# Longer unused matmuls, an earlier load of pair 3 and later values of pair 4 in the head of an attention and MLP kernel

## The chip, the core and the metric

The kernel runs on one core of one Trainium2 chip. The metric is the device time of one execution in microseconds (us), as the median of several runs. The core has a matrix engine (TensorE, PE in the profile), a vector engine (VectorE, DVE), an engine for activation functions (ScalarE, ACT), GpSimd (POOL) and SyncE (SP). POOL, SP and ACT can issue DMAs; all of them are served by the same 16 DMA engines of the core.

## The reference

The inputs are q, k and v of shape (8, 8, 576, 64), that is 8 batches, 8 heads, 576 positions and 64 columns, and 16 further keys and values per head (the beacons). All are float32. The result of the attention is laid out as 4608 tokens of 512 columns and goes through two layers of 512 to 2048 to 512 with a leaky ReLU between them.

```python
k_all = np.concatenate([beacon_k, k], axis=2)
v_all = np.concatenate([beacon_v, v], axis=2)
scores = scale * np.matmul(q, k_all.transpose(0, 1, 3, 2))
causal[:, Nb:] = np.triu(np.ones((S, S), dtype=bool), k=1)
scores = np.where(causal, -1000000000.0, scores)
scores = scores - scores.max(-1, keepdims=True)
a = np.exp(scores)
a /= a.sum(-1, keepdims=True) + 1e-09
...
h = x @ w_in
g = np.maximum(0.01 * h, h)
return (g @ w_out).astype(np.float32)
```

## The kernel before

**The units of work.** Attention is done by pairs of heads: 32 pairs, four to a batch, numbered 0 to 31. The keys of a pair, beacons included, are five blocks of up to 128 rows. The scores are computed with the keys on the partitions; ScalarE takes the exponential out of PSUM into a tile `aT`; GpSimd writes zeros over the triangle above the diagonal (`mask`, `triangle`); a further matmul with V, which carries a column of ones, gives the weighted values and their sum at once (`value`, line 342), and VectorE divides. The results are turned into `xT`, which the MLP reads: `moe1` (line 395) is the first layer and `moe2` (line 433) the second. An MLP step is four matmuls of 512 columns.

**An order written by hand.** All five engines run in the order in which the program names the work (`manual_schedule`). The head of the program is a handful of strings of short steps, which `run` reads. The steps that matter here:

- `lG.W` loads queries (W = 0) or keys (W = 1) of pair G into a raw tile (line 145, on POOL's queue). Each descriptor moves 2304 bytes in and 1152 out.
- `VB.C` loads block C of V of batch B (line 200, POOL's queue), `iN` and `oN` half of the weights of the first and the second layer (lines 118 and 124), `NG.W` queries or keys of pair G in natural layout (line 157), all on POOL's queue. V and N move pieces of 128 bytes into SBUF.
- `qG` and `kG` turn the raw tile of pair G on TensorE by 18 small matmuls with the identity (line 229) and copy the result out of PSUM; `TG` turns the natural layout by DMAs that SP issues (line 165).
- `sG.N` is part N of the scores of pair G and its exponential (lines 253 and 262), `mG.N` the masks (line 275), `vG.H` half H of the values, `xG` and `yG` turn the values on TensorE or by SP's DMAs, `u` and `d` are one MLP step of the first or the second layer.
- `wN` is N unused matmuls (line 486), 128 columns each, of a tile `blank` of zeros into a PSUM tile that nobody reads. `WG.H.N` is N unused matmuls of 112 columns (line 492) into spare columns of the tile that `vG.H` will write.

Later scores, from pair 8 on, are packed into full PSUM tiles (`stretch`, line 297), and a loop over timed events interleaves them with the MLP.

**Waits that come from the order.** POOL issues its DMAs in order, and they share eight semaphores in turn, so each DMA on POOL's queue waits until the one eight before it has landed. The issue of the first half of the first layer's weights (`i0`, line 118) is the sixteenth, behind V0.1, the eighth. The masks stand behind `i0` on POOL. The scores use two PSUM tiles, so a score waits for the exponential of the score two before it. TensorE is in order too: in the head, `s2.2` stands behind the turning of pair 3's queries, `q3`, though it does not use them.

Of the kernel before, what the change touches and what calls it, by code (L numbers as in the profile page):

```python
# [15 lines left out]
def kernel(  # L16
# [11 lines left out]
    nc = tc.nc  # L28
# [59 lines left out]
    blank = singles.tile([128, 128], BF16, name="blank")  # L88
# [54 lines left out]
    def load_qk(g, which):  # L143
        b, hp, grp, rows = where(g)
        loaded["qk", g, which] = nc.gpsimd.dma_start(  # L145
            out=raw_of(b, grp)[which][rows],
            in_=(q, k)[which][b, 2 * hp : 2 * hp + 2].rearrange("h (p i) d -> p h i d", i=RI),
        )
# [42 lines left out]
    def load_v_cast(b, c):  # L191
        dst = v_bufs[b % 2]
        lo = 0
        if c == 0:
            nc.gpsimd.dma_start(
                out=dst[0:NB, 0, :, 0:D], in_=beacon_v[b].rearrange("h p d -> p h d")
            )
            lo = NB
        n = ROWS[c] - lo
        nc.gpsimd.dma_start(  # L200
            out=dst[lo : ROWS[c], c, :, 0:D],
            in_=v[b, :, OFF[c] : OFF[c] + n].rearrange("h p d -> p h d"),
        )
# [38 lines left out]
    def score(g, n):  # L242
        qT, kT = qk[g]
        if n == 0:
            probs[g] = a_bufs[g % NA]
        aT = probs[g]
        parts = SCORES[n]
        sc = ps_sc.tile([128, 2, 512], FP32, name="sc", tag="sc")
        c0 = parts[0][3]
        for c, q0, w, col in parts:  # L250
            for par in range(2):
                ps_ = slice(par * 64, par * 64 + 64)
                nc.tensor.matmul(  # L253
                    out=sc[:, par, col - c0 : col - c0 + w],
                    lhsT=kT[ps_, c * 128 : (c + 1) * 128],
                    rhs=qT[ps_, q0 : q0 + w],
                    start=True,
                    stop=True,
                    skip_group_check=True,
                )  # L260
        w = sum(p[2] for p in parts)
        nc.scalar.activation(  # L262
            out=aT[:, :, c0 : c0 + w], in_=sc[:, :, 0:w], func=AF.Exp, scale=0.125
        )
# [3 lines left out]
    def mask(g, part):  # L268
        aT = probs[g]
        for lo, n, rows in MASKS[part]:  # L270
            triangle(aT, lo, n, rows)
# [210 lines left out]

    def unused(n, cols=128):
        ps = ps_one.tile([128, 512], FP32, name="av", tag="one")
        for i in range(n):
            nc.tensor.matmul(out=ps[:, 0:cols], lhsT=blank, rhs=blank[:, 0:cols], start=True, stop=True)  # L486

    def unused_ahead(g, half, n):
        if (g, half) not in avs:
# [17 lines left out]
    def finish(g, eng=0):  # L507
        if eng < 2 and g in xs:
            x_transposes(g, (dve, act)[eng])
        ready[0] = chunks_with(g)  # L510
        if g % NPAIR == NPAIR - 1:
            turn[0] = 1
            held[0] = KEPT

    def run(steps):
        for step in steps.split():
            op, a = step[0], [int(x) for x in step[1:].split(".")] if step[1:] else []
            if op == "s":
                score(*a)
            elif op == "m":  # L520
                mask(*a)
            elif op == "v":
                value(*a)
            elif op == "x":
                finish(*a)
            elif op == "l":
                load_qk(*a)
            elif op == "V":
                load_v_cast(*a)
            elif op == "N":  # L530
                load_natural(*a)
            elif op == "T":
                turn_pair(a[0])
            elif op == "y":
                x_turn(a[0])
            elif op == "q" or op == "k":
                t_q(a[0], 0 if op == "q" else 1, (dve, act)[a[1] if len(a) > 1 else 0])
            elif op == "b":
                beacon_columns(a[0], (dve, act, pool)[a[1]])
            elif op == "u":  # L540
                up()
            elif op == "P":
                moe1_early(*a)
            elif op == "d":
                down()
            elif op == "w":
                unused(*a)
            elif op == "W":
                unused_ahead(*a)
            elif op == "i":  # L550
                load_w_in(a[0])
            elif op == "o":
                load_w_out(a[0])
            else:
                raise ValueError(step)
# [11 lines left out]
    with order:  # L567
        load_first_keys()
        load_beacon_k(0, 2, nc.scalar)
        nc.vector.memset(blank, 0.0)  # L570
        run("l0.0 l1.0")
        make_identity(nc, ident)
        make_ones()
        run("l1.1 l2.0 l2.1 V0.0 V0.1 V0.2 l3.0 l3.1 V0.3 V0.4 l4.0 l4.1 i0")
        make_pads()
        unused(25)
        cast_beacon_k(0, 2, nc.scalar.copy)
        beacon_transposes(0, 2)
        unused(13)
        nc.scalar.copy(out=k_nat0[:, :, 0], in_=first_k[:, 0])  # L580
        nc.vector.tensor_copy(out=k_nat0[:, :, 1], in_=first_k[:, 1])
        run("q0.1 k0 w6 s0.0 m0.0 w5 s0.1 q1 s0.2 m0.1 k1 w4 s0.3 m0.2")
        run("w6 s1.0 m1.0 q2 s1.1 k2 w6 s1.2 m1.1 w6 s1.3 m1.2 W0.0.4 s2.0 m2.0 W0.0.4 s2.1 q3 l5.0 l5.1 W0.0.2 s2.2 k3 v0.0 m2.1 s2.3 i1 m2.2 W0.1.4 s3.0 m3.0 v1.0 s3.1 v0.1 s3.2 v1.1 m3.1 l6.0 l6.1 s3.3 x0.1 m3.2")
        run("v2.0 l7.0 l7.1 q4 v2.1 V1.0 V1.1 x1 k4.1 v3.0 v3.1 x2.1 s4.0 s4.1 x3 m4.0 V1.2 V1.3 V1.4 u s4.2 u q5 s4.3 m4.1 m4.2 k5 u o0 u")
        load_beacon_k(2, B, nc.gpsimd)
        run("s5.0 s5.1 m5.0 u u s5.2 s5.3 m5.1 m5.2 o1 u q6 k6 u v4.0 u v4.1 s6.0 s6.1 m6.0 u y4 N8.0 N8.1 u s6.2 s6.3 m6.1 m6.2 u")
        cast_beacon_k(2, B, nc.gpsimd.tensor_copy)
        run("q7 u k7 u v5.0 u v5.1 y5 N9.0 s7.0 s7.1 m7.0 d v6.0 v6.1 d y6 T8 s7.2 s7.3 m7.1 m7.2 N9.1 T9")
        beacon_transposes(2, B)
        run("b8.2 b9.2 b10.2 b11.2 u v7.0 v7.1 d d d d N10.0 N10.1 V2.0 V2.1 V2.2 V2.3 V2.4 d d N11.0 N11.1 x7")  # L590


        CUTS = [(0, 512, 1024, 1536, 1664), (0, 384, 896, 1376, 1664), (0, 224, 736, 1248, 1664)]
        BLOCKS = [((0, 0),), ((0, 1),)], [((0, 2),), ((0, 3), (1, 0))], [((1, 1),), ((1, 2),)], [((1, 3), (2, 0)), ((2, 1),)], [((2, 2),), ((2, 3),)]
        FIRST = 2 * NPAIR

        def block(g0, i):
            for tile in BLOCKS[i]:
                stretch([(g0 + r, CUTS[r][n], CUTS[r][n + 1]) for r, n in tile])

        events = []
        for g in range(FIRST, NG):
            if g > FIRST + 3:
                events.append((g - 3.6, 0, run, ("N%d.0" % g,)))
                events.append((g - 3.1, 0, run, ("N%d.1" % g,)))
            if g > FIRST + 1:
                events.append((g - 2.0, 0, run, ("T%d" % g,)))
            if g > FIRST + 3:
                events.append((g - 1.9, 0, run, ("b%d.2" % g,)))
            events.append((g + 2.25, 3, value, (g, 0)))  # L610
            events.append((g + 2.62, 4, value, (g, 1)))
            events.append((g + 2.63, 5, x_turn, (g,)))
            if (g - FIRST) % 3 == 0:
                for i in range(5):
                    events.append((g + (0.31 if g == FIRST else 0.01) + 0.6 * i, 2, block, (g, i)))
        ends = [FIRST]
        for g in range(FIRST, NG):
            events.append((g + 3.5, 2, finish, (g, 2)))
            if g % NPAIR == NPAIR - 1:
                ends.append(g + 3.5)  # L620
        for b in range(3, B):
            for n in range(NKB):
                events.append((4 * b - 0.9 + 0.3 * n, 6, load_v_cast, (b, n)))
        events.sort(key=lambda e: e[:2])
        first_down[0] = 4
        w, d0 = 0, done1[0] + done2[0]
        for at, _, what, args in events:
            while w + 2 < len(ends) and at > ends[w + 1]:
                w, d0 = w + 1, done1[0] + done2[0]
            todo = 2 * NF * ready[0] - KEPT - d0  # L630
            aim = d0 + todo * (at - ends[w]) / (ends[w + 1] - ends[w])
            while done1[0] + done2[0] < aim and fill():
                pass
            what(*args)
        while done2[0] < NCH * NF:
            fill()
# [30 lines left out]
```

## Time and profile before

| | |
|---|---|
| median of 8 runs | 343.12 us (341.04 to 346.12) |
| the profiled execution | 343.88 us |
| span of its records | 342.2 us, that is 1.7 us less |
| TensorE busy | 331.3 us (97%) |
| unused matmuls of 128 columns (line 486) | 71 |
| DMA engines | busy in nearly every slice until about 257 us |

The times of instructions are given from the start of the span. A busy TensorE is not TensorE at its peak, since matmuls overlap in the records. The granted clock of TensorE over the span is 0.987 of full speed, and all of the missing share is in a short stretch of the head and at the very end.

### The profile page before, as it was taken

How to read it: one execution, taken by the hardware profiler on the slowest of the kernel's cores; microseconds unless marked ns; L12 is line 12 of the kernel's file. 1: busy time of each engine (PE TensorE's matmuls, PEld its weight loads, DVE VectorE, ACT ScalarE, POOL GpSimd, SP SyncE). 2: the span in 40 equal slices, each digit the busy share in tenths (PEclk: the TensorE clock that was granted, in tenths of full speed). 3: DMA queues.
4: the chain of work that ended last, by engine and by line, in shares of the span. 5: the costliest groups of instructions: out<-in, count | busy, mean ns of one | idle time of the engine just before them, and what ended most of it. 6: DMA issues, size and time to landing. Idle time of an engine off the chain costs nothing.

```text
span 342.2 us, 7376 instructions
## 1 busy us (share of the span) xinstructions
PE 331.3 (97%) x2936; PEld 169.7 (50%) x2981; DVE 81.9 (24%) x199; ACT 186.6 (55%) x280; POOL 181.1 (53%) x355
## 2 busy tenths in 40 slices
PE   8799999989999999999999999999999999999995
PEld 7575555434544545454454454544545544444442
DVE  3355334211233113311232113212321220000111
ACT  4867872469645874288347852775447205633300
POOL 8696877959997685398466955682211000000000
PEclk9969999999999999999999999999999999999998
DMA  8999999999999999999999999999220130000021
GB/s 134 127 193 193 122 192 153 198 153 162 160 157 192 161 136 119 147 127 140 120 151 117 123 143 120 148 134 81 83 81 18 25 103 33 0 31 33 31 92 61
DMA packets 154322, 40.16 MB, mean 117 GB/s; under 512 B 144384, under 2 KB 148608, under 8 KB 154288
## 3 DMA queue, kind: packets, MB, share of 16 engines
q0 software_dynamic: 100848, 18.54, 78.6%
q1 hardware_dynamic: 53024, 20.96, 33.0%
q8 instruction: 23, 0.38, 0.5%
q10 hardware_dynamic: 416, 0.20, 0.2%
q14 instruction: 11, 0.09, 0.1%
HBM read 37.22 MB, written 9.44 MB: 136 GB/s over the span
## 4 chain that ended last, share of the span: by engine, by line
PE 87%; DMA 5%; POOL 5%; issue 1%; DVE 0%; ACT 0%; POOLq 0%
PE acc L395 35%; PE acc L433 33%; PE av L342 9%; PE sc L297 6%; DMA v_aug<-in_v_dram 3%; DMA q_raw<-in_q_dram 2%; PE sc L253 2%; POOL v_aug L200 1%; PE tp L229 1%; POOL k_nat L157 1%; POOL aT L275 1%; POOL q_raw L145 0%; POOL q_nat L157 0%; PE tp L364 0%; POOL k_raw L145 0%
## 5 line engine op out<-in xcount | busy, mean ns | idle before, releaser
L395 PE MATMUL acc<-xT,w_in_sb 128*128 128x512 bf16 x552 | 134.8, 379 | 1.2 <-issue 0.2
L433 PE MATMUL acc<-w_out_sb,gT 128*128 128x512 bf16 x555 | 132.3, 379 | 1.2 <-issue 0.2
L402 ACT ACTIVATE gT<-acc 128x512 bf16<-128x512 f32 x144 | 84.6, 607 | 63.6 <-PE acc L395 61.8
L310 ACT ACTIVATE aT<-sc 128x1024 bf16<-128x1024 f32 (+3 forms) x96 | 76.8, 867 | 62.5 <-PE sc L297 58.9
L275 POOL TENSOR_SCALAR_AFFINE_SELECT aT<-aT 128x256 bf16<-128x256 bf16 (+2 forms) x160 | 57.7, 388 | 64.8 <-ACT aT L310 52.9
L433 PEld LDWEIGHTS <-gT 128*128 128x128 bf16 x576 | 53.4, 98 | 61.2 <-issue 2.5
L395 PEld LDWEIGHTS <-w_in_sb 128*128 128x128 bf16 x576 | 52.6, 98 | 60.0 <-issue 2.7
L351 DVE RECIPROCAL rec<-av 128x6 f32<-128x6 f32 (+1 forms) x64 | 12.1, 188 | 142.5 <-PE av L342 142.5
L445 DVE COPY osb<-acc 128x512 f32<-128x512 f32 x35 | 24.2, 691 | 85.0 <-PE acc L433 78.6
L342 PEld LDWEIGHTS <-aT 128*128 128x128 bf16 (+1 forms) x960 | 37.1, 99 | 13.5 <-issue 3.4
L342 PE MATMUL av<-v_aug,aT 128*128 128x65 bf16 (+1 forms) x960 | 41.1, 196 | 0.1
L157 POOL DMA_DIRECT2D k_nat<-in_k_dram x48 | 34.8, 731 | 3.6 <-DMA v_aug<-in_v_dram 2.6
L157 POOL DMA_DIRECT2D q_nat<-in_q_dram x48 | 34.8, 731 | 2.2 <-DMA v_aug<-in_v_dram 0.9
L200 POOL DMA_DIRECT2D v_aug<-in_v_dram x40 | 34.0, 857 | 3.0 <-DMA w_in_sb<-in_moe_w_in_dram 2.7
L352 DVE TENSOR_TENSOR x_nat<-av,rec 128x384 bf16<-128x384 f32 (+1 forms) x64 | 31.4, 491 | 2.2
L262 ACT ACTIVATE aT<-sc 128x1024 bf16<-128x1024 f32 (+3 forms) x32 | 26.5, 879 | 6.6 <-PE sc L253 6.6
L297 PE MATMUL sc<-qT,kT 64*128 64x208 bf16 (+16 forms) x368 | 24.4, 255 | 1.4 <-POOL aT L275 1.1
L297 PEld LDWEIGHTS <-kT 64*128 64x128 bf16 x368 | 12.3, 94 | 20.2 <-issue 16.7
L253 PE MATMUL sc<-qT,kT 64*128 64x80 bf16 (+4 forms) x96 | 10.8, 302 | 0.0
L235 DVE COPY qT<-tp 128x576 bf16<-128x576 bf16 x7 | 5.3, 756 | 17.2 <-PE tp L229 17.2
L486 PE MATMUL av<-blank 128*128 128x128 bf16 x71 | 7.3, 270 | 1.1 <-DVE blank L570 1.1
L451 ACT COPY osb<-acc 128x256 f32<-128x256 f32 x1 | 0.4, 372 | 13.7 <-DVE osb L449 13.7
(44 smaller groups left out, 69.5 us busy)
## 6 DMA issues: line engine op xcount, KB each, us to landing
out_dram<-osb SPq DMA_DIRECT2D x35, 256.0 KB, 2.4
q_nat<-in_q_dram POOLq DMA_DIRECT2D x48, 72.0 KB, 4.2
k_nat<-in_k_dram POOLq DMA_DIRECT2D x48, 72.0 KB, 4.6
v_aug<-in_v_dram POOLq DMA_DIRECT2D x24, 128.0 KB, 5.8
w_in_sb<-in_moe_w_in_dram POOLq DMA_DIRECT2D x2, 1024.0 KB, 11.3
w_out_sb<-in_moe_w_out_dram POOLq DMA_DIRECT2D x2, 1024.0 KB, 12.4
q_raw<-in_q_dram POOLq DMA_DIRECT2D x8, 144.0 KB, 7.9
k_raw<-in_k_dram POOLq DMA_DIRECT2D x7, 144.0 KB, 8.6
```

Of the source, the lines that this page charges most:

```text
L157: nc.gpsimd.dma_start(out=t[:, :, par], in_=(q, k)[which][b, 2 * hp + par].rearrange("(t p) d -> p t d", p=NR),)
L200: nc.gpsimd.dma_start(out=dst[lo : ROWS[c], c, :, 0:D], in_=v[b, :, OFF[c] : OFF[c] + n].rearrange("h p d -> p h d"),)
L262: nc.scalar.activation(out=aT[:, :, c0 : c0 + w], in_=sc[:, :, 0:w], func=AF.Exp, scale=0.125)
L275: nc.gpsimd.affine_select(out=view, in_=view, compare_op=ALU.is_ge, fill=0.0, base=128 - n if lo == 0 else 0, channel_multiplier=-1, patte ...
L297: nc.tensor.matmul(out=sc[:, par, at : at + b - a], lhsT=kT[ps_, c * 128 : (c + 1) * 128], rhs=qT[ps_, q0 : q0 + b - a], start=True, stop= ...
L310: nc.scalar.activation(out=probs[g][:, :, lo:hi], in_=sc[:, :, at : at + hi - lo], func=AF.Exp, scale=0.125)
L342: nc.tensor.matmul(out=avv[:, n, 0 : D + 1], lhsT=aT[0 : ROWS[c], par, a0 : a0 + 128], rhs=va[0 : ROWS[c], c, 2 * hp + par, :], start=(c = ...
L352: nc.vector.tensor_tensor(out=x_nat[:, t0:t1].rearrange("p t e d -> p (t e) d"), in0=avv[:, :, 0:D], in1=rec[:, n0:n1, None].to_broadcast( ...
L395: nc.tensor.matmul(out=acc, lhsT=w_in_sb[:, j, fc * 128 : (fc + 1) * 128], rhs=xT[:, j, i * 512 : (i + 1) * 512], start=(j == 0), stop=(j ...
L402: nc.scalar.activation(out=gT[i][:, fc, :], in_=acc, func=AF.Prelu, alpha=0.01)
L433: nc.tensor.matmul(out=acc, lhsT=gT[i][:, fc, t * 128 : (t + 1) * 128], rhs=w_out_sb[:, fc, :], start=(fc == 0), stop=(fc == NF - 1),)
L445: nc.vector.tensor_copy(out=osb, in_=acc)
```

## The change

Three things change in the head; nothing after pair 7 is touched.

1. The unused matmuls take more columns each. `unused` repeats the 128 columns of `blank` by a step of zero, so that one matmul streams 256, 384 or 512 columns. In place of 71 matmuls with 128 columns there are 23, with their 23 weight loads: 25 x 128 becomes 6 x 512, 13 x 128 becomes 6 x 256, `w6` and `w5` become 2 x 384, and `w4` becomes 1 x 512.
2. The loads of pair 3's queries and keys (`l3.0 l3.1`) stand on POOL's queue ahead of the third block of V (`V0.2`), not behind it. With it, two unused matmuls `W0.0.2` stand ahead of `q3`, not between the keys' load of pair 5 and `s2.2`.
3. The values of pair 4 (`v4.0 u v4.1`) stand behind the first scores of pair 6 (`s6.0 s6.1 m6.0`), not ahead of them.

```diff
     def unused(n, cols=128):
         ps = ps_one.tile([128, 512], FP32, name="av", tag="one")
+        r, w = max(1, cols // 128), min(cols, 128)
         for i in range(n):
-            nc.tensor.matmul(out=ps[:, 0:cols], lhsT=blank, rhs=blank[:, 0:cols], start=True, stop=True)
+            nc.tensor.matmul(
+                out=ps[:, 0 : r * w].rearrange("p (r w) -> p r w", w=w),
+                lhsT=blank,
+                rhs=blank[:, None, 0:w].to_broadcast([128, r, w]),
+                start=True,
+                stop=True,
+            )
...
-        run("l1.1 l2.0 l2.1 V0.0 V0.1 V0.2 l3.0 l3.1 V0.3 V0.4 l4.0 l4.1 i0")
+        run("l1.1 l2.0 l2.1 V0.0 V0.1 l3.0 l3.1 V0.2 V0.3 V0.4 l4.0 l4.1 i0")
         make_pads()
-        unused(25)
+        unused(6, 512)
         cast_beacon_k(0, 2, nc.scalar.copy)
         beacon_transposes(0, 2)
-        unused(13)
+        unused(6, 256)
...
-        run("q0.1 k0 w6 s0.0 m0.0 w5 s0.1 q1 s0.2 m0.1 k1 w4 s0.3 m0.2")
-        run("w6 s1.0 m1.0 q2 s1.1 k2 w6 s1.2 m1.1 w6 s1.3 m1.2 W0.0.4 s2.0 m2.0 W0.0.4 s2.1 q3 l5.0 l5.1 W0.0.2 s2.2 k3 v0.0 m2.1 s2.3 i1 m2.2 W0.1.4 s3.0 m3.0 v1.0 s3.1 v0.1 s3.2 v1.1 m3.1 l6.0 l6.1 s3.3 x0.1 m3.2")
+        run("q0.1 k0 w2.384 s0.0 m0.0 w2.384 s0.1 q1 s0.2 m0.1 k1 w1.512 s0.3 m0.2")
+        run("w2.384 s1.0 m1.0 q2 s1.1 k2 w2.384 s1.2 m1.1 w2.384 s1.3 m1.2 W0.0.4 s2.0 m2.0 W0.0.4 s2.1 W0.0.2 q3 l5.0 l5.1 s2.2 k3 v0.0 m2.1 s2.3 i1 m2.2 W0.1.4 s3.0 m3.0 v1.0 s3.1 v0.1 s3.2 v1.1 m3.1 l6.0 l6.1 s3.3 x0.1 m3.2")
...
-        run("s5.0 s5.1 m5.0 u u s5.2 s5.3 m5.1 m5.2 o1 u q6 k6 u v4.0 u v4.1 s6.0 s6.1 m6.0 u y4 N8.0 N8.1 u s6.2 s6.3 m6.1 m6.2 u")
+        run("s5.0 s5.1 m5.0 u u s5.2 s5.3 m5.1 m5.2 o1 u q6 k6 u u s6.0 s6.1 m6.0 v4.0 u v4.1 y4 N8.0 N8.1 u s6.2 s6.3 m6.1 m6.2 u")
```

## The prediction

> **What bounds the kernel now.** I read the page first: TensorE is busy 97% of the span, so anything that shortens TensorE's work or its idle time counts, and little else does. But the share is a mean. The row of the granted clock has one bad place:
>
> ```profile
> PE 331.3 (97%) x2936; PEld 169.7 (50%) x2981; DVE 81.9 (24%) x199; ACT 186.6 (55%) x280; POOL 181.1 (53%) x355
> ...
> PEclk9969999999999999999999999999999999999998
> ```
>
> The third slice (17.1 to 25.7 us) has 6 tenths. Cut into pieces, the columns being busy time of each engine, then the clock:
>
> ```profile
> 5.70:9.10 3.40, 3.37 (x83) 2.40 (x82) 1.49 (x3) 2.39 (x4) 3.40 (x5) 1.00 1.33 146
> 9.10:12.50 3.40, 3.40 (x75) 2.28 (x70) 2.31 (x4) 3.36 (x6) 3.01 (x5) 1.00 2.01 137
> 12.50:15.95 3.45, 1.78 (x21) 0.88 (x18) 0.00 (x0) 3.07 (x4) 1.23 (x3) 1.00 2.91 125
> 15.95:19.40 3.45, 3.32 (x61) 2.37 (x62) 1.92 (x4) 0.94 (x2) 3.45 (x11) 0.50 1.48 148
> 19.40:22.80 3.40, 3.40 (x40) 2.17 (x40) 1.18 (x4) 2.54 (x3) 3.39 (x8) 0.50 1.11 202
> ```
>
> The third piece is where TensorE is busy only 1.78 of 3.45 us, and just after it the clock is half for 6.8 us. The chain of waits over the first 30 us names what it waits for:
>
> ```profile
> 5.51 2.54 POOL v_aug L200 x3
> 8.05 7.99 DMA q_raw<-in_q_dram
> 16.04 0.04 issue
> 16.08 0.69 PE tp L229 x18
> ```
>
> Pair 3's queries are issued at 8.05 us, behind three blocks of V, and land at 16.04. TensorE idles from 14.28 (end of `s2.1`) to 16.08, 1.8 us. ScalarE runs out at the same time: its ten exponentials end at 15.58 and the next starts at 17.58.
>
> The second thing to see is far behind the change. From 7 us on, the DMA engines always have packets, and TensorE meets them again at the first scores of pair 8 and at 75 us (timeline: start, duration, what, and in brackets the idle time before it; the line with 4.7 is an answer on DMAs, time to landing last):
>
> ```profile
> 57.86 1.20 SPq L165 DMA_TRANSPOSE kT<-k_nat  x1
> ...
> kT<-k_nat SPq DMA_TRANSPOSE x1, 4.7
> ...
> 62.62 0.36 PEld L297 LDWEIGHTS <-kT 64*128 64x128 bf16 x6 [0.59 <-issue]
> ...
> 72.98 1.44 POOL L157 DMA_DIRECT2D k_nat<-in_k_dram  x2 [2.57 <-DMA v_aug<-in_v_dram]
> ...
> 75.50 0.49 PE L297 MATMUL sc<-qT,kT 64*128 64x224 bf16 x6 [1.09 <-POOL aT L275]
> ```
>
> 57.86 + 4.7 = 62.56: pair 8's turned keys land just as TensorE loads them, after 0.59 us of waiting. So at 62.6 us TensorE has no slack towards the DMAs, and at 75.5 it waits 1.09 us more.
>
> **Part 1, longer unused matmuls.** 71 matmuls of 128 columns become 23; 48 matmuls and 48 weight loads go. That is no time by itself: the columns are what costs. The timeline has 25 weight loads of `blank` in 2.59 us at the start, 104 ns each, and at 6.47 us six in 0.34 us, 57 ns each. So a 128-column step takes the time of its columns, first at a slow clock and then at a full one; the weight loads lie beside the matmuls. A matmul of 512 columns with a step of zero is not in the trace; the nearest row is first-layer MLP work, twelve matmuls of 512 columns in 2.59 us, 216 ns each at the full clock, which is four times 54. I take the same price per column; the ends are 6 x 216 = 1.3 us (were the clock full) and 6 x 456 = 2.7 us (the 2.85 us of the matmul row / 25 x 4) against my 6 x 416 = 2.5. Columns: the first two fills go from 38 x 128 = 4864 to 4608, so 256 fewer, 2 x 104 = 0.2 us earlier; the queries of pair 0 landed at 5.34 and are turned at 5.70, so these 0.2 us can be had. `w5` gains 128 columns, +0.05 us, beside the exponentials, which take 8.23 us without a gap from 7.35 and pace everything to 15.58. Sum: **0.15 us** earlier.
>
> **Part 2, pair 3 ahead of V0.2.** Landing times from the answers on DMAs (issue plus time to landing): V0.1 about 14.4, V0.2 15.5, queries 16.04, keys 8.64 + 8.6 = 17.24, V0.3 19.0, V0.4 19.9. They land in the order of issue although issued 0.6 to 0.9 us apart with 8 us of latency, so they stand in one line[...]. Without V0.2 in front, pair 3 saves V0.2's step, 15.5 − 14.4 = 1.1 us: queries at about 15.0, keys at 16.2. V0.2 then lands when all three had landed, 17.24. The ends: 16.04 still (if what holds the line is V0.1's slow engine and the others' traffic), and 0.87 us earlier issue plus the 4.9 us that pair 1 needed in a short line, 12.1. I take 15.0.
>
> TensorE then has `W0.0.2` (0.1 us) and idles about 0.6 us, not 1.8. `s2.2` follows at 15.4, its exponential at 15.8, not 17.58. `k3` ends near 16.7. **The new wait:** `v0.0` needs V0.2 (17.24) and holds the in-order TensorE for 0.5 us, with `s2.3` behind it; before, it started at 18.08, so this is still earlier. V0.3 and V0.4 keep their places: `v0.1` (21.51 before) cannot start its last part before 19.9, and at most 1.6 us are to be had there. On POOL, `i0` waits for V0.1 as before (14.72), so the masks behind it start at 15.50 as before; `v0.0` needs three of them, 16.7. `l5.0` waits on the semaphore of pair 3's queries instead of V0.2's, both long landed by 19.2.
>
> **The clock.** From 16.08 to 22.69 the chain's pieces sum to 6.6 us. The same kinds of pieces after 23 us take: 18 turnings 0.40 (against 0.69), 12 values 0.37 (0.78), 18 values 0.66 (1.10), unused 0.2 (0.49). At a full clock the sum would be 4.0 us, up to 2.6 less, of which V0.4 lets about 1.6 to 2.0 through. Would the clock stay? Here the Trainium skill ("TensorE: Matmul & The Clock Gate", "Why this matters for your kernels") says to avoid idle gaps over about 3 us. By that rule a gap of 1.8 us is harmless, the change touches no cause, and this part is worth the 0.8 us below. The row differs: after 1.78 busy of 3.45 us the clock was 0.50, so the measurement decides that a shorter gap can matter. Against the change speaks Part 4 of the same page, that turning on TensorE does not count as busy: 36 of the small matmuls now in 15 to 17 us are turnings, and the piece 15.95 to 19.40, full by the row (3.32 of 3.45) and rich in them, did not raise the clock. With the clock kept the head gains about 2.0 us, with it lost 0.8 (1.0 earlier, less a wait on V0.2). I take it as even, 1.4 us, plus 0.15.
>
> **Part 3, values of pair 4.** V1.4 is issued at 34.6, lands at 40.3, and `v4.1` starts at 40.12, its last block used near 40.5: slack 0.2. With a head 1.5 us earlier it would wait 1.3 us. The move puts `s6.0 s6.1` (0.58 us) and one MLP step (0.86) ahead, 1.44 us, so the wait goes. POOL's order is the same: `N8` stays behind `m6.0`, whose exponentials come a little sooner. SP's three turnings by DMA (`y4` to `T8`) keep their order. Cost nothing; without it, up to 1.3 us.
>
> **The sum.** TensorE reaches MLP work 1.5 us earlier (28.42 to 26.9; the weights land at 14.72 + 11.3 = 26.0, not late). It keeps that until 62.6 us. There pair 8's keys come from the natural loads issued at 44.5 and landed at 56.9 and 57.3, in line behind the two weight loads, on DMA engines that never ran dry; these do not come sooner, so **TensorE waits away the 1.5 us at 62.6**. What survives is on POOL: its loads from 54.9 on (pairs 9 to 11, V of batch 2) follow masks, so they move ahead with TensorE, and DMA time of a load is only 4 to 5 us there, so the line is short. The 1.09 us of waiting at 75.5, behind V2's landing, can shrink. I take half, 0.6 us. The profiled execution took 343.88; 343.3 after. It stands 0.8 above the median 343.12, so on the median: **342.5 us**.
>
> **Rivals.**
> - *The whole gain is carried* (0.25): the line of DMAs moves up as TensorE does, since POOL's issues after 21 us are tied to masks. For it: latencies fall to 4 us at 57. Against it: packets in every slice. Gain 2.2 us (2.0 + 0.15): 340.9, and 339.4 if other runs are hit harder than the profiled one.
> - *Nothing is gained* (0.16): the clock falls all the same and 62.6 and 75.5 are set by DMA: 343.1.
> - *Slower, V0.2 takes pair 3's place* (0.12): if V0.2 falls back to V0.4's landing, 19.9, `v0.0` starts 1.8 us later than 18.08, TensorE idles 3 us, and one more piece of 3.4 us runs at half clock, 1.7 us. It decides from a landing of V0.2 later than 18.1. 343.1 + 3.5 = 346.6.
> - *The longer fills do not hold the clock*: since columns are equal, I give it no chance of its own; it would show as the second rival.
>
> **How the numbers follow.** The likeliest case (0.47) is the partial gain, 342.5. The range goes from the far end of the first rival, with some room, 339.6, to 345.6, short of the slower one. About 1% is what a measurement of this kernel can tell from no change: under 339.7, over 346.5. Faster by over 1% is only the end of the first rival (0.12); slower most of the last (0.10); within, 0.78.
>
> **What would show it.** Right: queries of pair 3 turned at about 15 us; an idle gap under 1 us ahead of them; `v0.0` waiting on V0.2 near 17.2; first MLP step near 27; idle time before the weight load of pair 8's keys near 2 us instead of 0.59, and less than 1.09 at 75. Wrong: turning still at 16, or keys of pair 8 landing well before 62, which would mean that the DMAs do follow and the gain is whole.

## The result and the profile after

The changed kernel takes **346.47 us** (median of 20 executions, 342.87 to 347.92, one at 560.54 aside) against 343.2 us of 55 executions of the kernel before on the same chip: a ratio of **1.0091**, 95% interval 1.0069 to 1.0114. It is slower by almost 1%, where the forecast was 342.5 us. Ratios here and below rest on undisturbed executions only, so they can differ from the quotient of the two medians shown. The profiled execution took 347.37 us with a span of 345.6 us, 3.4 us more than the span before.

The page of the changed kernel, the rows of busy time and of the granted clock:

```profile
PE 331.9 (96%) x2888; PEld 165.4 (48%) x2933; DVE 81.8 (24%) x199; ACT 186.2 (54%) x280; POOL 181.4 (52%) x355
...
PEclk9999999699999999999999999999999999999999
```

The 48 matmuls are gone and TensorE's busy time is the same. The place with 6 tenths has moved from the third slice to the eighth. The pieces of the head (start and end, length, busy time of PE, PEld, DVE, ACT and POOL, then clock, DMA share, GB/s) have no hole any more where it was:

```profile
12.50:15.95 3.45, 3.45 (x75) 2.21 (x74) 1.27 (x2) 3.45 (x5) 3.45 (x10) 1.00 2.31 135
15.95:19.40 3.45, 3.45 (x72) 2.46 (x69) 2.48 (x9) 3.45 (x6) 3.45 (x8) 1.00 1.28 180
19.40:22.80 3.40, 2.96 (x91) 2.62 (x88) 2.98 (x9) 1.73 (x3) 3.39 (x10) 1.00 1.12 206
```

So the head did what the change says. The timeline of TensorE (start, duration, what) has pair 3's queries turned at 14.17 us with no wait in front, and V0.2 was there for `v0.0` at 15.26:

```profile
14.17 0.47 PE L229 MATMUL tp<-ident,q_raw 64*64 64x64 bf16 x18
14.57 0.35 PE L253 MATMUL sc<-qT,kT 64*128 64x336 bf16 x4
14.86 0.47 PE L229 MATMUL tp<-ident,k_raw 64*64 64x64 bf16 x18
15.26 0.54 PE L342 MATMUL av<-v_aug,aT 128*128 128x65 bf16 x12
```

The first MLP step starts at 24.56 us, 3.9 earlier than in the profile before. This row of the changed kernel, then that of the kernel before:

```profile
24.56 1.08 PE L395 MATMUL acc<-xT,w_in_sb 128*128 128x512 bf16 x3
```

```profile
28.46 1.08 PE L395 MATMUL acc<-xT,w_in_sb 128*128 128x512 bf16 x3
```

All of it is gone by pair 8, and more. A first part goes at 52 us, in a wait for the second half of `w_out`; when TensorE is done with the work ahead of pair 8, at 60.77 us where the kernel before was at 62.53, 1.76 us of the lead are left. The same timeline there and at the first scores of pair 8 (line 297); in brackets the idle time before a row and what ended it:

```profile
53.44 5.34 PE L433 MATMUL acc<-w_out_sb,gT 128*128 128x512 bf16 x23 [1.34 <-DMA w_out_sb<-in_moe_w_out_dram]
...
58.88 1.89 PE L433 MATMUL acc<-w_out_sb,gT 128*128 128x512 bf16 x8
64.59 1.03 PE L297 MATMUL sc<-qT,kT 64*128 64x512 bf16 x6 [3.82 <-DMA kT<-k_nat]
65.56 1.89 PE L433 MATMUL acc<-w_out_sb,gT 128*128 128x512 bf16 x4
67.24 1.91 PE L395 MATMUL acc<-xT,w_in_sb 128*128 128x512 bf16 x4
69.37 1.26 PE L433 MATMUL acc<-w_out_sb,gT 128*128 128x512 bf16 x3 [0.22 <-issue]
70.47 1.03 PE L395 MATMUL acc<-xT,w_in_sb 128*128 128x512 bf16 x4
71.43 0.63 PE L297 MATMUL sc<-qT,kT 64*128 64x16 bf16 x12
```

The first and the second scores of pair 8 in the kernel before:

```profile
62.65 0.61 PE L297 MATMUL sc<-qT,kT 64*128 64x512 bf16 x6
...
66.75 0.64 PE L297 MATMUL sc<-qT,kT 64*128 64x16 bf16 x12
```

In the changed kernel TensorE stands still for 3.82 us in one piece, and an MLP step that takes 1.03 us at 70.47 takes 1.9 us from 65.56 to 69. The pieces show the clock:

```profile
60.00:63.40 3.40, 0.77 (x4) 0.15 (x2) 0.00 (x0) 0.00 (x0) 3.29 (x6) 1.00 1.84 156
63.40:70.30 6.90, 5.49 (x17) 2.05 (x19) 0.00 (x0) 2.54 (x3) 6.24 (x11) 0.51 1.84 193
```

TensorE is busy for 0.77 us of 3.40, and the clock is half for the next 6.8 us, two pieces of 3.4. The sum of the profiled execution: the first scores of pair 8 come 64.59 − 62.65 = 1.94 us later than before; the second ones come 71.43 − 66.75 = 4.68 later, so the stretch at half clock costs 2.74 more; behind them 1.3 us come back, since the wait of 1.09 us at 75.5 is gone. 1.94 + 2.74 − 1.3 = 3.4 us, the difference of the spans.

Why pair 8's turned keys were late is in the chain of waits (start, duration, what):

```profile
40.97 18.18 DMA k_nat<-in_k_dram
59.16 0.00 issue
59.16 0.03 SPq L165
59.19 0.04 issue
59.22 5.23 DMA kT<-k_nat
```

The natural loads were issued 3.9 to 4.2 us earlier than before and were in the line for 18.2 us, not 12.1, so they landed 1.8 us later. The answers on DMAs, first of the kernel before, then of the changed one (last number: us from issue to landing):

```profile
q_nat<-in_q_dram POOLq DMA_DIRECT2D x2, 72.0 KB, 12.5
k_nat<-in_k_dram POOLq DMA_DIRECT2D x2, 72.0 KB, 12.1
```

```profile
q_nat<-in_q_dram POOLq DMA_DIRECT2D x2, 72.0 KB, 18.1
k_nat<-in_k_dram POOLq DMA_DIRECT2D x2, 72.0 KB, 18.2
```

Counted over the packets of the trace, the DMA engines had moved 7.51 MB by 45 us, 0.5 MB more than before; by 60 us they had moved 9.52 MB, a little less than the 9.60 MB of before. In two stretches they moved little:

```profile
40.00:45.00 5.00, 4.89 (x70) 2.63 (x69) 2.03 (x4) 3.54 (x6) 3.09 (x7) 1.00 1.14 192
45.00:48.00 3.00, 3.00 (x56) 1.95 (x54) 1.09 (x5) 2.34 (x3) 2.27 (x4) 1.00 1.68 63
48.00:50.00 2.00, 1.94 (x32) 1.08 (x30) 1.02 (x3) 0.62 (x2) 0.41 (x1) 1.00 1.19 193
...
55.00:57.00 2.00, 2.00 (x11) 0.92 (x10) 0.69 (x1) 0.00 (x0) 0.00 (x0) 1.00 1.77 69
57.00:60.00 3.00, 3.00 (x20) 1.47 (x18) 1.05 (x2) 0.00 (x0) 2.70 (x4) 1.00 2.34 151
```

63 and 69 GB/s, where the pieces beside them have 150 to 195. That was not for want of work: the column ahead of the rate, packets under way per engine, says 1.68 and 1.77 there.

### The profile page after: what moved, and what is told of

Same layout as the page of the kernel before. It is cut to its first block, busy times and chain, and to the rows that moved or that the text cites. A ratio compares the mean times of both kernels' runs of the same rounds, so it can differ in the third digit from the quotient of the medians.

```text
span 345.6 us, 7280 instructions
## 1 busy us (share of the span) xinstructions
PE 331.9 (96%) x2888; PEld 165.4 (48%) x2933; DVE 81.8 (24%) x199; ACT 186.2 (54%) x280; POOL 181.4 (52%) x355
## 4 chain that ended last, share of the span: by engine, by line
PE 82%; DMA 10%; POOL 5%; issue 1%; DVE 0%; ACT 0%; SPq 0%
PE acc L433 34%; PE acc L395 32%; PE av L342 7%; PE sc L297 6%; DMA k_nat<-in_k_dram 5%; DMA w_in_sb<-in_moe_w_in_dram 3%; POOL aT L275 2%; PE av L487 2%; DMA kT<-k_nat 2%; POOL v_aug L200 1%; PE tp L229 1%; PE sc L253 1%; POOL q_nat L157 0%; POOL k_raw L145 0%; POOL w_out_sb L124 0%
## 5 line engine op out<-in xcount | busy, mean ns | idle before, releaser
L402 ACT ACTIVATE gT<-acc 128x512 bf16<-128x512 f32 x144 | 84.7, 607 | 67.2 <-PE acc L395 65.5
L433 PEld LDWEIGHTS <-gT 128*128 128x128 bf16 x576 | 53.7, 98 | 63.8 <-issue 5.8
L395 PEld LDWEIGHTS <-w_in_sb 128*128 128x128 bf16 x576 | 52.9, 98 | 60.4 <-issue 3.6
L351 DVE RECIPROCAL rec<-av 128x6 f32<-128x6 f32 (+1 forms) x64 | 12.1, 188 | 142.2 <-PE av L342 142.2
L342 PEld LDWEIGHTS <-aT 128*128 128x128 bf16 (+1 forms) x960 | 36.3, 98 | 14.3 <-issue 3.0
L253 PE MATMUL sc<-qT,kT 64*128 64x80 bf16 (+4 forms) x96 | 10.1, 284 | 0.0
L487 PE MATMUL av<-blank 128*128 128x384 bf16 (+2 forms) x23 | 7.1, 434 | 1.1 <-DVE blank L577 1.1
```

What stands on the lines that cost most here:

```text
L342: nc.tensor.matmul(out=avv[:, n, 0 : D + 1], lhsT=aT[0 : ROWS[c], par, a0 : a0 + 128], rhs=va[0 : ROWS[c], c, 2 * hp + par, :], start=(c = ...
L395: nc.tensor.matmul(out=acc, lhsT=w_in_sb[:, j, fc * 128 : (fc + 1) * 128], rhs=xT[:, j, i * 512 : (i + 1) * 512], start=(j == 0), stop=(j ...
L402: nc.scalar.activation(out=gT[i][:, fc, :], in_=acc, func=AF.Prelu, alpha=0.01)
L433: nc.tensor.matmul(out=acc, lhsT=gT[i][:, fc, t * 128 : (t + 1) * 128], rhs=w_out_sb[:, fc, :], start=(fc == 0), stop=(fc == NF - 1),)
```

## The experiments

**The theory.** The head gains time, but pair 8's keys come when the DMA line gives them, not sooner. The lead collects there as one wait, and the clock halves behind it, which costs more than the lead is worth. **The rivals:** one of the three parts is slow by itself; part 3 does harm by sending pair 8's loads and the turnings of pairs 5 and 6 into the line earlier; the one profiled execution was unlucky. The last runs add two: the place of TensorE's code loads, and a clock that rises late.

| run | what differs from the kernel before | median us | ratio to before, 95% interval |
|---|---|---|---|
| changed kernel | parts 1, 2, 3 | 346.47 | 1.0091, 1.0069 to 1.0114 |
| e1 | part 1 | 343.82 | 0.9993, 0.9965 to 1.0020 |
| e2 | part 2 | 343.12 | 0.9986, 0.9955 to 1.0018 |
| e6 | part 3 | 343.63 | 0.9978, 0.9951 to 1.0005 |
| e5 | parts 1, 2 | 344.38 | 1.0030, 1.0002 to 1.0059 |
| e15 | parts 2, 3 | 344.08 | 1.0008, 0.9980 to 1.0036 |
| e3 | all, wait at pair 8 filled with unused matmuls | 344.63 | 1.0043, 1.0020 to 1.0066 |
| e4 | all, pairs 5 and 6 turned on TensorE | 341.78 | 0.9959, 0.9936 to 0.9982 |
| e8 | only pairs 5 and 6 turned on TensorE | 342.78 | 0.9985, 0.9960 to 1.0011 |
| e16 | parts 2, 3, pairs 5 and 6 on TensorE | 341.32 | 0.9964, 0.9946 to 0.9982 |
| e11 | all, pairs 4, 5, 6 turned on TensorE | 341.84 | 0.9948, 0.9925 to 0.9971 |
| e7 | all, turnings of pairs 5 and 6 behind pair 8's | 349.10 | 1.0126, 1.0074 to 1.0179 |
| e12 | all, pair 8's loads ahead of half of `w_out` | 348.33 | 1.0161, 1.0113 to 1.0210 |
| e17 | all, opening's unused matmuls as before | 345.25 | 1.0075, 1.0046 to 1.0104 |
| e18 | all, other unused matmuls as before | 346.22 | 1.0035, 0.9998 to 1.0072 |

e9, e10, e13 and e14 are one profiled execution each, told below.

### One part at a time

Part 1 alone, e1 (`unused` as changed):

```diff
-        unused(25)
+        unused(6, 512)
...
-        run("q0.1 k0 w6 s0.0 m0.0 w5 s0.1 q1 s0.2 m0.1 k1 w4 s0.3 m0.2")
+        run("q0.1 k0 w2.384 s0.0 m0.0 w2.384 s0.1 q1 s0.2 m0.1 k1 w1.512 s0.3 m0.2")
...
```

> Part 1 alone (fewer and longer unused matmuls), all else as before. Theory A (the head becomes shorter, TensorE then starves at the first scores of pair 8, which wait for keys that come through the DMA engines at a time of their own, and the long idle time halves the clock for 6.8 us): part 1 moves the head by only 0.2 us, so the time is that of before, 343.2 within 1 us, and the half-clock stretch stays in the head at 16 us. Theory B (the three parts do no harm by themselves; the profiled run met an accidental standstill of the DMA engines of about 3 us at 45 us, and that is what is measured): the same. Theory C (matmuls with a step of zero are themselves the cost): slower, 345 or more.

Part 2 alone, e2:

```diff
-        run("l1.1 l2.0 l2.1 V0.0 V0.1 V0.2 l3.0 l3.1 V0.3 V0.4 l4.0 l4.1 i0")
+        run("l1.1 l2.0 l2.1 V0.0 V0.1 l3.0 l3.1 V0.2 V0.3 V0.4 l4.0 l4.1 i0")
...
```

> Part 2 alone (pair 3's queries and keys ahead of the third block of V, and two unused matmuls ahead of their turning). Theory A: this part alone makes the head 3 to 4 us shorter and so carries the loss: 345.5 to 347, idle time of 3 us or more in front of pair 8's scores at about 64 us and half clock behind it. Theory B: the head is shorter too, and without a standstill the time is at or under that of before, 340 to 343. Theory C: as before, 343.

Part 3 alone, e6, and parts 1 and 2 without it, e5:

```diff
-... o1 u q6 k6 u v4.0 u v4.1 s6.0 s6.1 m6.0 u y4 N8.0 ...
+... o1 u q6 k6 u u s6.0 s6.1 m6.0 v4.0 u v4.1 y4 N8.0 ...
```

> Part 3 alone, the head as before. Theory A2: without the shorter head nothing waits for V at the values of pair 4 (0.2 us of slack in the profile of before), so the move changes little: 342.5 to 344. Theory D (the order of the values of pair 4 is bad by itself, whatever the head): 345 to 347.

> Parts 1 and 2 together, values of pair 4 where they stood before. Theory A2 (part 3 is what turns the shorter head into a loss: without it TensorE waits for the last blocks of V of batch 1 in front of the values of pair 4, some 2 us in small pieces near 38 us, as in the run with part 2 alone, so the turnings by DMA of pairs 5 and 6 are issued later and pair 8's natural loads land sooner): 342.5 to 344, pair 8's keys turned from 55 to 57 us, no wait over 1.5 us there. Theory A (the shorter head alone makes the loss, and the run with part 2 alone was spared by chance): 345.5 to 347.

Each part alone is within the uncertainty of no change. Together they are slower, so the loss is an interaction: no part is slow by itself. Parts 1 and 2 carry about a third of it, and part 3 on top of them the rest (1.0030 to 1.0091). The median of e5, 344.38 us, falls between the two ranges expected for it. Parts 1 and 3 together were not run.

The single profiles do not support the theory as it was put for e1 and e2. In e2 the first MLP step starts at 25.08 us, 3.4 earlier than in the profile before, and 345.5 us or more were expected for that. But 2.0 us go in waits for V at 36 to 38 us, the waits that part 3 was to take away, and the scores of pair 8 follow without any:

```profile
61.82 0.61 PE L297 MATMUL sc<-qT,kT 64*128 64x512 bf16 x6
```

The profile of e1 is that of its slowest execution, 349.04 us, one that its ratio leaves out. Pair 8's natural loads were issued there at 42.7 us as in the kernel before, so they had no lead, and TensorE came to pair 8 later than before, at 63.51. Yet the keys came so late that the same wait stands there, with half clock for one piece behind it:

```profile
67.33 0.61 PE L297 MATMUL sc<-qT,kT 64*128 64x512 bf16 x6 [3.82 <-DMA kT<-k_nat]
```

So in these profiles a lead of the head is neither enough for this wait nor needed for it.

### The wait, and what it does to the clock

e3 keeps the whole change and puts unused work where TensorE would stand still, just ahead of pair 8's first scores:

```diff
+        events.append((FIRST + 0.305, 1, unused, (16, 512)))
```

> The changed kernel with 16 more unused matmuls of 512 columns (16 x 0.216 = 3.5 us at the full clock) right before the first scores of pair 8, that is, inside the wait of 3.8 us. Theory A: the wait for the keys stays, but the clock stays up behind it; the 6.8 us at half clock go, worth about 2.7 us: 343.5 to 344.5 instead of 346.5. Theory B: nothing gained, 346.5, or slower by what the fill overruns. Theory C: 16 more such matmuls make it slower.

The median falls from 346.47 to 344.63 us, just above the 343.5 to 344.5 expected, and the ratio from 1.0091 to 1.0043. In its profile the clock stays full from 5.9 us to the end, and the timeline has a short wait left:

```profile
65.30 0.61 PE L297 MATMUL sc<-qT,kT 64*128 64x512 bf16 x6 [0.72 <-DMA kT<-k_nat]
```

So about half of the loss was the half clock, got back by work that nobody needs. The rest is not told apart: the row of the 16 matmuls has 3.62 us in the profile, so where the keys are not that late, the filling itself costs.

The mean clocks of the single executions agree, though a mean does not tell where the half clock stood. Of 19 executions of the changed kernel 11 have a mean clock of 0.9925 or less (two pieces of 3.4 us at half clock) with a median of 347.25 us, five about 0.995 (one piece) with 345.91, and three 0.998 or more with 343.65. Of 55 of the kernel before in the first set of experiments, 16% are in the first class and 35% in the second; of all 22 of e3 none is under 0.994. Half a clock for 6.8 us is 3.4 us of lost work; 347.25 − 343.65 is 3.6.

### Sparing the DMA engines

e4 turns the values of pairs 5 and 6 on TensorE (`x`), where SP's DMAs did it (`y`); e8 does this alone in the kernel before.

```diff
-... v5.1 y5 N9.0 s7.0 s7.1 m7.0 d v6.0 v6.1 d y6 T8 ...
+... v5.1 N9.0 s7.0 s7.1 m7.0 x5 d v6.0 v6.1 d x6 T8 ...
```

> The changed kernel with the values of pairs 5 and 6 turned by TensorE (0.4 us each on an engine that idles later anyway) instead of by four DMAs of SP, which are in flight between 46 and 60 us together with the natural loads of pair 8. Theory A: less stands in front of pair 8's loads, its keys land 1 to 2.5 us sooner, TensorE waits 1.5 to 3 us instead of 3.8, and where the clock holds the time is 342 to 344. Theory B: the standstill comes or does not come as in the changed kernel, so 346.5 within 1 us.

> The kernel before (none of the three parts) with the values of pairs 5 and 6 turned by TensorE instead of by SP's DMAs. The changed kernel with the same edit took 341.78. If the change has a gain of its own once pair 8's loads are freed, this one lies above it: 342.5 to 343.5, since its head is 3 us longer and TensorE reaches pair 8 at 62 us anyway. If the gain was that of the turning alone: 341.8 within 0.7.

With it the loss is gone: 0.9959 in place of 1.0091, and 341.78 us, under the 342 to 344 expected. Without any of the three parts it is 0.9985; since the two intervals overlap, whether the three parts add to the gain is not shown. In e4's timeline pair 8's transposes leave SP at 52.89, not 57.88, and the scores follow without a wait:

```profile
60.74 0.61 PE L297 MATMUL sc<-qT,kT 64*128 64x512 bf16 x6
```

The clock was full there (0.998 over the span). In all four profiles with these turnings on TensorE (e4, e8, e11, e16) the transposes leave SP between 52.1 and 52.9 us. In the others, but for the three in which the clock rose late (below), they leave between 53.5 and 60.5. e16 is e4 without part 1, e11 turns pair 4 on TensorE as well (`x4`, one MLP step behind the place of `y4`):

> Parts 2 and 3 with pairs 5 and 6 turned by TensorE, the unused matmuls of the head as before. With part 1 the same kernel had a ratio of 0.9959 to before. Theory (part 1 gives a lead that is kept once pair 8's keys are early): 0.9965 to 0.999. Rival (part 1 costs by late lifts of the clock): 0.992 to 0.9955.

> The changed kernel with the outputs of pairs 4, 5 and 6 turned by TensorE (with a vector copy) and not by the DMA engines. Theory (the DMA engines are the bound up to pair 8's keys, and every turning that they are spared brings the keys sooner, at 0.5 to 0.7 us of TensorE for each pair): with pairs 5 and 6 on TensorE the median was 341.8, so a third pair saves little more, since no wait on the keys over 0.7 us is left: 341.2 to 342.3. Rival (TensorE's cost of a turning decides): 342.4 to 343.2.

e16 falls between the two ranges expected: 0.9964 beside 0.9959, so where the keys are early, part 1 is worth nothing that can be seen, neither a gain nor a cost. e11 is where the theory put it, with the lowest ratio of all, 0.9948, though its interval overlaps e4's.

### Moving pair 8 in the line

e7 leaves the turnings to the DMAs but puts those of pairs 5 and 6 behind pair 8's on SP:

```diff
-... v5.1 y5 N9.0 s7.0 s7.1 m7.0 d v6.0 v6.1 d y6 T8 ...
+... v5.1 N9.0 s7.0 s7.1 m7.0 d v6.0 v6.1 d T8 y5 y6 ...
```

> The changed kernel with the turnings by DMA of the values of pairs 5 and 6 behind those of pair 8's queries and keys on SP's queue; same instructions, and TensorE's order is untouched. Theory A2 (it is the early turnings of pairs 5 and 6 that stand between pair 8's loads and their landing): pair 8 is turned from 53 to 55 us instead of 57.9, TensorE's wait falls from 3.8 to under 1.5 us, 341.5 to 343.5. Theory B (a standstill of the DMA engines made the loads late): as the changed kernel, 346.5 within 1 us.

The time missed. The timeline shows that the part on the keys held and that the wait went elsewhere:

```profile
61.09 0.61 PE L297 MATMUL sc<-qT,kT 64*128 64x512 bf16 x6 [0.22 <-DMA kT<-k_nat]
...
65.42 0.55 PE L395 MATMUL acc<-xT,w_in_sb 128*128 128x512 bf16 x1 [2.53 <-DMA xT<-x_nat]
69.31 1.03 PE L395 MATMUL acc<-xT,w_in_sb 128*128 128x512 bf16 x2 [3.35 <-DMA xT<-x_nat]
```

The scores of pair 8 come 3.5 us sooner than in the changed kernel. But the MLP needs what was pushed back, waits 5.9 us for it in two pieces, and the clock is half from 65.5 to 72.3 us. e12 moves the loads themselves:

```diff
-... m5.1 m5.2 o1 u q6 k6 u u s6.0 s6.1 m6.0 v4.0 u v4.1 y4 N8.0 N8.1 u ...
+... m5.1 m5.2 N8.0 N8.1 o1 u q6 k6 u u s6.0 s6.1 m6.0 v4.0 u v4.1 y4 u ...
```

> The changed kernel with the two loads of pair 8's queries and keys issued ahead of the second half of w_out and not five steps behind it. Theory A (the loads land late because everything issued ahead of them has to land first, 18 us in the line): pair 8's turned keys come 3 us or more sooner, first scores of pair 8 without a wait on DMA, and the second half of w_out lands 2 to 4 us later, so that the first down steps wait for it instead: 344 to 348. Theory B (the turnings of pairs 5 and 6 that share the engines set the landing, not the place in the line): the transposes of pair 8 are issued at 56 to 58 as in the changed kernel, 346 to 348 and a wait on kT<-k_nat over 2.5 us.

Theory A is right on the loads, which land in 7.7 and 9.7 us in place of 18, and on the second half of `w_out`, which is late instead:

```profile
59.32 3.15 PE L433 MATMUL acc<-w_out_sb,gT 128*128 128x512 bf16 x7 [4.76 <-DMA w_out_sb<-in_moe_w_out_dram]
```

It is wrong on the keys: their transpose leaves SP 3.5 us sooner than in the changed kernel but is under way for 9.2 us and lands at 64.88, no sooner than there (64.45).

```profile
55.68 2.90 SPq L165 DMA_TRANSPOSE kT<-k_nat  x1
```

No wait is left at pair 8 only because TensorE comes there later, after the wait on `w_out`. The time is just over the 344 to 348 expected.

In both moves another thing became late. Only kernels with transfers taken out of the line (e4, e11, e16) gained anything clear of their intervals. That fits a DMA line that sets the pace up to about 60 us.

### More profiles of both kernels

> The kernel before as it is, for a second profiled execution. Theory: the clock falls to half either in the head (wait for pair 3's queries, 1.8 us in the first profile) or at the scores of pair 8, but not for 6.8 us at the latter; the first scores of pair 8 at 61.5 to 63.5 with a wait under 2 us; 341.5 to 344. Rival (pair 8's keys come as late here as in the changed kernel): first scores of pair 8 at 64 or later.

The kernel before again, 344.33 us: pair 8 at 63.85 us after 1.17 us of waiting, and no half clock before the end, though one was expected in the head or at pair 8.

```profile
63.85 0.61 PE L297 MATMUL sc<-qT,kT 64*128 64x512 bf16 x6 [1.17 <-DMA kT<-k_nat]
```

Its first MLP step stood at 26.87, not 28.46: the half clock in the head of the first profile belongs to that execution.

> The changed kernel as it is, for a second profiled execution. Theory (the head is some 3 us sooner, pair 8's turned keys are not, and the difference stands in one piece ahead of the scores of pair 8): the first MLP step again at 24.5 to 26, the first scores of pair 8 at 63.5 or later after a wait of over 2.5 us on DMA kT<-k_nat, the clock half for 3.4 or 6.8 us behind it, 345 to 348 us. Rival (the one profiled execution was unlucky: the standstill of the DMA engines from 45 to 48 us made pair 8's keys late): without a standstill between 40 and 58 us the keys are there by 62, the wait is under 1.5 us and the time 343 to 344.

> The changed kernel as it is, for one more profiled execution; the second one had TensorE at its lower clock up to 26.9 us and told nothing of pair 8. Theory (the lead of the head stands as one piece of idle time ahead of pair 8): first MLP step at 24.5 to 26, a wait of over 2.5 us on DMA kT<-k_nat, the clock half for 3.4 or 6.8 us behind it, 345 to 348 us. Rival (that wait was the luck of one execution): a wait under 1.5 us, no half clock near 60 to 70, 342.5 to 344.5. Second rival (long unused matmuls leave the clock low for long in the head): full clock first at 10 us or later, first MLP step at 28 or later.

> As the third profile, once more: the first theory holds if at least two of the four profiles of the changed kernel show the wait of over 2.5 us with half clock behind it; the second rival if full clock comes first at 10 us or later in two of them.

Two of the four profiles of the changed kernel, the first and e14, show the wait of over 3 us with half clock behind it. In e14 it was half for one piece, and the time, 344.28 us, was under the 345 to 348 expected:

```profile
63.03 1.04 PE L297 MATMUL sc<-qT,kT 64*128 64x512 bf16 x6 [3.63 <-DMA kT<-k_nat]
```

```profile
62.40:65.80 3.40, 2.77 (x11) 1.04 (x12) 0.00 (x0) 1.94 (x2) 3.20 (x5) 0.50 1.94 166
```

The other two, e9 (346.85) and e13 (346.35), have a quite different trouble: full clock only from 27 us on. The first scores of 512 columns of the changed kernel, then of e9:

```profile
6.69 0.39 PE L253 MATMUL sc<-qT,kT 64*128 64x512 bf16 x2
```

```profile
7.52 0.61 PE L253 MATMUL sc<-qT,kT 64*128 64x512 bf16 x2
```

Their first MLP step comes at 32 us and pair 8's keys are then in time. So both conditions set ahead of e14 are met. The lists of clocks tell that this second trouble is not what the measured 346.47 rests on: no execution there is over 344.9 us at a clock of 0.998 or more, as e9 and e13 are.

### Which part carries it

> Parts 2 and 3 without part 1: the unused matmuls of the head have 128 columns as before. Theory (the head's lead makes the loss, and the lead came of parts 1 and 2 together with the clock kept up): lead about 2 us smaller than in the changed kernel, wait on pair 8's keys 1.5 to 2.5 us, ratio 0.998 to 1.004. Rival (part 3's order of v4 makes the loss, by issuing pair 8's loads and the turnings of pairs 4 and 5 into the line earlier): the changed kernel's loss without part 1, ratio 1.006 to 1.011. Second rival (part 1 alone makes it, by its late lifts of the clock): ratio 0.996 to 0.999.

Parts 2 and 3 alone give 1.0008: **without part 1 there is no loss to be seen**, and part 3's order is not enough for it. Its profile has no wait to speak of at pair 8, where 1.5 to 2.5 us were expected. e17 and e18 take part 1 back by halves:

```diff
-        unused(6, 512)
+        unused(25)
...
-        unused(6, 256)
+        unused(13)
```

> The changed kernel, with only the opening's unused matmuls (before the first queries are turned) back at 25 and 13 of 128 columns: 26 matmuls and 26 weight loads more, no unused work more between scores. Theory A (the lead that the long unused matmuls between the scores give is what stands at pair 8): lead and wait as in the changed kernel, ratio 1.006 to 1.011. Theory B (the place of TensorE's code loads: one of 16 KB for about each 256 instructions of TensorE; with part 1 they fall at 54 to 56 us, where pair 8's loads land and are turned, without it at 51 to 53): 52 instructions more move the loads some 1.6 us ahead, to 44 to 45 and 52.5 to 53, standstills of the DMA engines between 53 and 58 us get rarer, ratio 1.000 to 1.005. Theory C (the long opening leaves the clock low up to 27 us in some executions): no late rise here, ratio 1.000 to 1.005 as with B, but with the code loads' place making no difference in e18.

```diff
-        run("q0.1 k0 w2.384 s0.0 m0.0 w2.384 s0.1 q1 s0.2 m0.1 k1 w1.512 s0.3 m0.2")
+        run("q0.1 k0 w6 s0.0 m0.0 w5 s0.1 q1 s0.2 m0.1 k1 w4 s0.3 m0.2")
...
```

> The changed kernel, with the opening as changed (6 of 512 and 6 of 256 columns) and only the unused matmuls between the scores back at 128 columns (w6, w5, w4): 20 matmuls and 20 weight loads more. Theory A: the lead is back near that of the kernel without part 1 (first MLP step at 26 to 26.5), wait on pair 8's keys under 2.5 us, ratio 0.998 to 1.004. Theory B: 40 instructions more move the code loads some 1.3 us ahead: ratio 1.001 to 1.006, and a little above that of e17. Theory C: late rises of the clock stay, ratio 1.006 to 1.011.

e17 keeps the loss, and its profile the wait, at a place where the code load had moved to 53.1 us as theory B wanted:

```profile
64.45 0.90 PE L297 MATMUL sc<-qT,kT 64*128 64x512 bf16 x6 [3.80 <-DMA kT<-k_nat]
```

By its ratio and its wait that speaks for theory A and against B and C. e18's 1.0035 is at the upper end of A, but it fits B as well, and it rests on six executions. Its eight others took 346.0 to 347.1 us, five of them at a mean clock of 0.999 or 1.0 as e9 and e13 did, and its profile is one of the late clock (full from 27.1 us). The median of all fourteen is 1.1% above the kernel before, which is what C expected, so e18 does not rule C out for the opening. Nor does theory A explain all of e17: its first MLP step stands at 26.39 us, that of e15 at 26.28, TensorE comes to pair 8 at 60.65 and 60.34, and yet pair 8's transposes leave SP at 57.68 in the one and at 53.67 in the other. **It is the keys that come late, and not only a lead that is waited away.** How part 1, which touches no DMA, delays them stays open.

## Why the prediction was wrong

- **Part 1, "0.15 us earlier".** In time by itself right: the opening took 2.74 us against 2.85, six matmuls of 512 columns at 457 ns, the upper end given. That it would have no other effect was wrong: with parts 2 and 3 it makes the difference between 1.0008 and 1.0091.
- **Part 2, landings.** Under-sized. The queries landed 5.5 us after their issue at 7.18, so at 12.7 and not 15.0; this was near the lower end, 12.1. V0.1 landed at 12.1, not 14.4. There was no wait on V0.2 near 17.2.
- **The clock in the head.** Taken as even; it stayed full. The head's lead was 3.9 us against the profile before and, since that one was hit in the head, 1.9 us between e10 and e14. The 1.5 us forecast were near the latter. The rule that TensorE's turnings don't count as busy changed nothing here: the piece 15.95 to 19.40 was full and the clock with it.
- **Part 3, "cost nothing".** Held alone: e6 is 0.9978. With parts 1 and 2 it makes the difference between 1.0030 and 1.0091, which the sum did not have.
- **"TensorE waits away the 1.5 us at 62.6".** The mechanism was seen, and this is **the step that failed**: the wait was entered at its own length, as if it could only eat the lead. It was 3.82 us and not 2.1. The lead left at that place, 1.76 us, was near the 1.5 forecast, but pair 8's loads did not land as before but 1.8 us later, and the turned keys 1.94; and behind the wait the clock was half for 6.8 us. The prediction had used the half clock behind 1.8 us of idle time for the head and did not apply it to the idle time that it forecast itself. The two omitted terms are 1.94 and 2.74 us in the profile; by e3 the clock is worth about half of the loss of the median. Why the keys came later is open. "These do not come sooner" should have been "at what spread do they come": over the profiles with full clock in the head, the transposes leave SP between 52.8 and 57.9 us.
- **75.5 us.** Right in kind: the 1.09 us of waiting went, 1.3 us came back, against 0.6 forecast.
- **The rivals.** "The whole gain is carried" is out. The slower rival had the right size, 346.6, and the wrong place: V0.2 landed in time. The range was too narrow on its upper side because the forecast wait was given no price beyond itself.

The Trainium skill ("TensorE: Matmul & The Clock Gate", "Why this matters for your kernels") asks for no gaps over about 3 us between bursts; 3.82, 3.63 and 3.80 us here all had half clock behind them, so the rule held where it was not applied. But it lets shorter gaps pass that had it too. In the 20 profiles TensorE idles nine times for 1.8 us or more between its first work and the end, and each time half clock follows (2.53 us is enough in e7, 1.80 in the kernel before); of twelve gaps of 1.0 to 1.7 us two have it. By these figures the 2.1 us that were forecast were already in danger.

## What to carry to other kernels

Before making the front of a kernel faster, find the first place where the fast engine meets the DMA line, and price the lead as one idle piece there: if wait plus lead come to 1.8 us or more, the shortest gap that always had it here, count one or two pieces of 3.4 us at half clock as well. Where the line is full, moving a load ahead only chooses what is late; take transfers off the line first (here the turnings of two or three pairs, for some 0.5 us of TensorE each), which took the whole loss away here. Three edits that each measure as nothing can add up to a loss, so try them together and one by one.

## What the hardware showed that was not expected

**DMA packets slow down together, around code loads.** In 19 of the 20 profiles there are stretches of 1.1 to 3.1 us in which packets that otherwise take 0.03 to 0.2 us take 1 to 2.9 us, many at once. Counted between 30 and 150 us, where at least 20 packets took over 1 us, there are 66; 61 of them begin from 1.5 us before to 2.0 us after a packet of 16 KB of the instruction queue starts, windows that cover 26 to 29% of the time. Between two such packets TensorE runs some 120 to 128 matmuls and 123 to 132 weight loads, that is about 250 instructions, which agrees with the 256 to a 16 KB line in the Trainium skill ("Advanced Engine Details and Errata", ISA Cache). So nearly every one of these stretches goes with a load of TensorE's code, though by no means every load with such a stretch, and which causes which is not shown. Ten of the profiles have one between 45 and 58 us, and all four waits of over 3 us on pair 8's keys (changed kernel, e1, e14, e17) are among them; in the ten without one that wait is at most 1.44 us (e6). This goes with the late keys more closely than the lead does, though five of the ten with one (e2, e5, e7, e12, e13) have hardly a wait there. Without part 1 one of these loads falls at 50.6 to 52.6 us; the 96 instructions less of part 1 put it at 54.3 to 57.9 where the clock was full early, onto the landing of pair 8's keys, and the turnings on TensorE of e4 and e11, instructions again, at 52.6 and 52.7. That fits the times, but e17 put it at 53.1 and kept the loss, with a stretch of slow packets at 53.7, so it is a suspicion and no cause.

**The clock can rise very late.** Three profiles (e9, e13, e18) had full clock only from 27 us on with TensorE busy in every piece from 1.2 us. All three have the long opening of part 1, as nine others that rose by 10.5 us have; none of the eight profiles with 128 columns in the opening rose later than 6.6 us. Three of twelve against none of eight can be chance, and 8 of 67 executions of the kernel before in the first set of experiments took 346.1 to 347.7 us at a mean clock of 0.998 or more, of which there is no profile. So it is not shown that the long opening is needed for it. The mean granted clock of these executions reads 0.999 to 1.0: the records begin with the rise, and only the durations of the rows (0.61 us against 0.39) show what came before.
